# Layer A of a two-layer attention kernel: fillers between the score visits in another order, the output stage two groups later, the next segment's layer norms in the first groups, exp of q read from SBUF

## The chip, the cores and the metric

The kernel runs on one core of a Trainium2 chip. The core has five engines that run side by side, each with its own instruction queue in program order: TensorE (PE in the profile; its weight loads are shown apart as PEld), VectorE (DVE), ScalarE (ACT), GpSimd (POOL) and SyncE (SP, which here only issues DMAs). The metric is the device time of one execution in microseconds (us), lower is better. Verdicts compare medians of several runs.

## The reference

Four layers in a row, A, B, A, B, each with a residual, on x of 2048 tokens by 640 features:

```
x = x + A(layernorm(x));  x = x + B(layernorm(x));  x = x + A(layernorm(x));  x = x + B(layernorm(x))
```

Layer A has 32 heads of 20 features. The tokens are cut into N = 4 segments of 512. Within a segment it is causal softmax attention; across segments there is a memory M, z that is read with phi(q) and updated with phi(k):

```
phi = lambda t: jnp.where(t > 0, t + 1.0, jnp.exp(t))
for s in range(N):
    p = _softmax(qs @ ks^T * scale + mask)
    a_dot = p @ vs
    a_mem = (phi(qs) @ M) / (phi(qs) @ z + 1e-06)
    o = g * a_mem + (1.0 - g) * a_dot
    M = M + phi(ks)^T @ vs ;  z = z + sum(phi(ks))
return o @ wo
```

Layer B is a recurrent-memory attention of 64 small steps. The change does not touch it.

## The kernel before

`layer_A` is called twice. It works through 4 segments (n) of 8 groups of four heads (G); the group counter is g = 8 n + G, from 0 to 31, with two more rounds to drain. Only the instructions of TensorE are held in the order in which the program writes them (`_OrdNC` with the engine "tensor"); the order on ACT, DVE and POOL is the tile scheduler's, which goes by the program's order where several instructions are ready. Tiles of a pool are given out as they come free.

**Score visits.** The heads of a group are done in two pairs p (`half`), and each pair in two visits (`ph`), so a group has four quarters (slots 0 to 3): a visit and then a few fillers. A visit works on up to three PSUM tiles of pool `psx` (three tiles of two banks, tag x):

- S tiles: the causal scores q k^T of the pair, for the row maximum alone. `s_mask` writes the mask with a product of the identity matrix, `s_mm` adds q k^T, `s_max` (line 400, DVE) reduces to the negated maximum `a_nm`. S0 has 1024 elements a partition, S2 512, and S1 768 and 256 in two reduces.
- T tiles: the scores once more, transposed and with the maximum subtracted (`a_q` holds q with the maximum in two extra rows), for the pair three places earlier (tp = p - 3). `t_round` does the products, `t_exp` (line 442, ACT) the exp into `a_PT`, and line 444 (POOL) clears what lies above the diagonal. T0 and T1 have 1024 elements, T2 512.

The products of a pair have 32 rows of contraction, at rows 32 j; the S pair and the T pair of a visit lie on different rows. Visits before: S0, T0, S2 and then T1, S1, T2.

**Fillers.** They do the rest of the layer for neighbouring groups. All their PSUM tiles come from pool `pg`, tag pg, which has two tiles, so a third product in a quarter needs the first to have been copied out.

- `proj_q` (QP): q of the next group; ACT copies it to `a_qT` (line 294); from segment 1 on also exp of q (`a_EQ`, line 298), and DVE makes phi(q) (lines 300, 302).
- `proj_kv` (KV0, KV1): k and v of the next group in two halves; ACT casts them to `a_Kn` and `a_vaug` (line 315). `k_turn` (KT): transpose of k; ACT copies it to `a_kT` (line 323). The S products of the next group need `a_kT`.
- `q_with_max` (Q2): q with the maxima; ACT copies it to `a_q` (line 416).
- `phi_k`: exp of k on ACT (line 332), POOL and DVE make `a_phik`. `state_up` (UP, segments 0 to 2): phi(k)^T v, evacuated on DVE (line 366, `a_upm`), added on POOL. `state_num` (NUM, segments 1 to 3): phi(q) M, copied by ACT to `a_nsb` (line 347).
- `pv` (PV): probabilities times v; ACT copies it to `a_osb` (line 459); `norm` puts the group's output into `a_Onat`.
- The output stage of the segment before, one block of 128 tokens a group in groups 2 to 5: `out_stage_a` (load of x, transpose `a_otps`, copy by ACT to `a_oT`, line 261) and `out_stage_b` in two halves (product with wo, `a_YP`, five matmuls of 320 columns; DVE adds x, line 275; after the second half two stores, line 278 and 281).
- For the next segment, for each of its four blocks: `seg_load` (DMA of x, line 231), `seg_norm` (layer norm: `layernorm_tile`, lines 76 to 83, on DVE with one power on POOL), `seg_tr` (transpose `a_tps`, copied by ACT, line 249). `seg_step` says in which (group, slot) each of the three is done.

Loads of x and stores of the result all go through SP's queue, in order. The output stage of the last segment runs after the loop.

Of the kernel before, what the change touches and what calls it, by code (L numbers as in the profile page):

```python
# [160 lines left out]
def layer_A(nc, tc, C, W, x_src, x_dst, src_is_bf16, nseg=4, out_bf16=False, xb_dst=None, load_w=None, side_loads=None):  # L161
# [6 lines left out]
    with ExitStack() as ctx:  # L168
# [116 lines left out]
        def proj_q(g):  # L285
            n, G = divmod(g, 8)
            s_ = GS[g] = {}
            xnT = SEG[n]["xnT"]
            wqG = W.wq[:, :, 4 * G:4 * G + 4, :].rearrange("p c h s -> p c (h s)")
            QP = pg.tile([128, 512], F32, name="a_QP", tag="pg")  # L290
            for c in range(NCH):
                nc.tensor.matmul(QP[:], lhsT=wqG[:, c, :], rhs=xnT[:, c, :], start=(c == 0), stop=(c == NCH - 1))
            qT = qp3.tile([128, 512], BF16, name="a_qT")
            nc.scalar.copy(qT[:], QP[:])
            s_["qT"] = qT
            if n >= 1:
                EQ = w1.tile([128, 512], BF16, name="a_EQ")
                nc.scalar.activation(out=EQ[:], in_=QP[:], func=ACT.Exp)
                rq = w1.tile([128, 512], BF16, name="a_rq")
                nc.vector.tensor_scalar(out=rq[:], in0=qT[:], scalar1=0.0, scalar2=None, op0=ALU.max)  # L300
                phiq = wk.tile([128, 512], BF16, name="a_phiq")
                nc.vector.scalar_tensor_tensor(out=phiq[:], in0=EQ[:], scalar=1.0, in1=rq[:], op0=ALU.min, op1=ALU.add)
                s_["phiq"] = phiq
# [14 lines left out]
        def k_turn(g):  # L318
            KT_ = pg.tile([128, 4, 128], BF16, name="a_KT", tag="pg")
            for tt in range(4):  # L320
                nc.tensor.transpose(KT_[:, tt, :], Kn[g % 2][:, tt, :, :].rearrange("p j s -> p (j s)"), C.identb[:])
            kT = qp4.tile([128, 512], BF16, name="a_kT")
            nc.scalar.copy(kT[:], KT_[:].rearrange("p t k -> p (t k)"))
            GS[g]["kT"] = kT
# [31 lines left out]
        def state_up(g):  # L356
            n, G = divmod(g, 8)
            s_ = GS[g]
            if n <= nseg - 2:
                UP = pg.tile([128, 128], F32, name="a_UP", tag="pg")  # L360
                pk, va = s_["pk"], s_["va"]
                for tt in range(4):
                    nc.tensor.matmul(UP[:], lhsT=pk[:, tt, :, :].rearrange("p j s -> p (j s)"),
                                     rhs=va[:, tt, :, :].rearrange("p j s -> p (j s)"), start=(tt == 0), stop=(tt == 3))
                upm = w1e.tile([128, 128], F32, name="a_upm")
                nc.vector.tensor_tensor(out=upm[:], in0=UP[:], in1=C.bdmask[:], op=ALU.mult)
                nc.gpsimd.tensor_tensor(out=MZ32[:, G, :], in0=MZ32[:, G, :], in1=upm[:], op=ALU.add)
                nc.gpsimd.tensor_copy(MZb[:, G, :], MZ32[:, G, :])
# [38 lines left out]
        def q_with_max(g):  # L407
            s_ = GS[g]
            N_ = NM[g % 2]
            Q2 = pg.tile([128, 512], F32, name="a_Q2", tag="pg")  # L410
            nc.tensor.matmul(Q2[:], lhsT=C.identb[:], rhs=s_["qT"][:], start=True, stop=False, skip_group_check=True)
            for qc in range(4):
                nc.tensor.matmul(Q2[:, 128 * qc:128 * qc + 128], lhsT=N_[:, qc, :, :].rearrange("p j s -> p (j s)"), rhs=C.identb[:],
                                 start=False, stop=(qc == 3), skip_group_check=True)
            q2 = wk.tile([128, 512], BF16, name="a_q2")
            nc.scalar.copy(q2[:], Q2[:])
            s_["q2"] = q2
# [73 lines left out]
        proj_kv(0, 1)  # L491
        k_turn(0)

        def seg_step(n, G, slot):
            if n + 1 >= nseg:
                return
            for tt, at in enumerate((((0, 0), (0, 2), (0, 3)), ((0, 3), (1, 1), (1, 3)), ((5, 2), (6, 0), (6, 1)), ((6, 0), (6, 2), (6, 3)))):
                for f, w_ in zip((seg_load, seg_norm, seg_tr), at):
                    if w_ == (G, slot):
                        f(n + 1, tt)  # L500

        def filler(g, slot):
            n, G = divmod(g, 8)
            out = n >= 1 and 2 <= G <= 5 and n <= nseg
            if slot == 0:
                if 0 <= g - 1 < NGR:
                    state_up(g - 1)
                if g + 1 < NGR:
                    proj_q(g + 1)
            elif slot == 1:  # L510
                if 0 <= g - 1 < NGR:
                    q_with_max(g - 1)
                if g + 1 < NGR:
                    proj_kv(g + 1, 0)
                if out:
                    out_stage_a(n - 1, G - 2)
            elif slot == 2:
                if g < NGR:
                    phi_k(g)
                    state_num(g)  # L520
                if g + 1 < NGR:
                    proj_kv(g + 1, 1)
                if out:
                    out_stage_b(n - 1, G - 2, (0,))
            else:
                if g + 1 < NGR:
                    k_turn(g + 1)
                if 0 <= g - 2 < NGR:
                    pv(g - 2)
                    norm(g - 2)  # L530
                if out:
                    out_stage_b(n - 1, G - 2, (1,))
            seg_step(n, G, slot)

        for g in range(NGR + 2):
            n, G = divmod(g, 8)
            for half in range(2):
                p, tp = 2 * g + half, 2 * g + half - 3
                for ph in range(2):
                    items = ((("S", 0), ("T", 0), ("S", 2)), (("T", 1), ("S", 1), ("T", 2)))[ph]  # L540
                    todo = []
                    for kind, r in items:
                        if kind == "S" and g < NGR:
                            todo.append((kind, p, r, s_mask(p, r)))
                        elif kind == "T" and 0 <= tp < 2 * NGR:
                            todo.append((kind, tp, r, t_tile()))
                    for kind, p_, r, X in todo:
                        (s_mm if kind == "S" else t_round)(p_, r, X)
                        (s_max if kind == "S" else t_exp)(p_, r, X)
                    if g < NGR and half == 1 and ph == 1:  # L550
                        negmax_rows(g)
                    filler(g, 2 * half + ph)
            if side_loads is not None and n == 0:
                if G == 0:
                    build_gates(nc, st, W, side_loads[1])
                side_loads[0](G, GS[g]["kT"])
# [671 lines left out]
```

## Time and profile before

| | |
|---|---|
| median of 3 runs | 2793.08 us (2786.16 to 2794.82) |
| the profiled execution | 2787.25 us, span 2785.5 us |
| mean granted TensorE clock | 0.981 |
| first A layer | about 0 to 405 us of the span |
| second A layer | about 1390 to 1790 us |

A group of layer A takes 8.4 to 14 us in segment 0, 9.7 to 12 us in segments 1 and 2, and 9.2 to 11.7 us in segment 3. The profile has a page (shares of each engine, the span in 40 slices, the chain that ended last, groups of instructions by line) and answers on parts of the trace: the busy time of each engine in a window, who waited for whom, and the instructions in order of time. Busy time of PE is modelled, since matmuls are pipelined; the start times are measured. A line "PE a_otps <- ACT a_q" in the list of waits says that the instruction of PE which writes a_otps was held until the instruction of ACT which writes a_q was done.

### The profile page before, as it was taken

The numbers are of one execution on the slowest core, as the hardware profiler recorded it, in microseconds if no ns is written. First come the engines' busy times: TensorE is split into PE (matmuls) and PEld (weight loads), VectorE is DVE, ScalarE is ACT, GpSimd is POOL, SyncE is SP. The second block draws the span as 40 slices with busy tenths as digits, with TensorE's granted clock in tenths as the row PEclk, the third lists the DMA queues.
The fourth block names the chain that finished last, engine by engine and source line by source line (L and its number), as shares of the span: only waits on it lengthen the run. The fifth ranks groups of instructions, "written<-read, shape, count | busy, mean of one in ns | idle before, by whom it ended". The sixth has DMA issues, their size and how long they took to land. (4 is left out here: it accounts for less than half of the span.)

```text
span 2785.5 us, 146956 instructions
## 1 busy us (share of the span) xinstructions
PE 2574.7 (92%) x65414; PEld 1700.1 (61%) x65480; DVE 1686.6 (61%) x4553; ACT 1584.9 (57%) x3708; POOL 715.2 (26%) x1645
## 2 busy tenths in 40 slices
PE   5888879999999999999978888799999999999998
PEld 3555556666666666666645555556666666666665
DVE  6888854555555555555578888445555555555554
ACT  4888854555555555544458888445555455555443
POOL 4666541111111111111146665411111111111110
PEclk9999979999999999999989999899999999999999
DMA  6111162221212212111120111721211121211110
GB/s 239 41 44 40 30 195 69 45 46 41 45 43 45 43 43 45 43 39 30 41 99 28 51 49 37 231 47 39 42 42 40 40 44 40 43 41 38 39 26 20
DMA packets 322300, 156.36 MB, mean 56 GB/s; under 512 B 245760, under 2 KB 310400, under 8 KB 318592
## 3 DMA queue, kind: packets, MB, share of 16 engines
q1 hardware_dynamic: 320224, 136.47, 19.2%
q8 instruction: 512, 8.39, 1.3%
q10 hardware_dynamic: 1440, 10.49, 1.0%
q14 instruction: 124, 1.02, 0.1%
HBM read 95.15 MB, written 51.71 MB: 53 GB/s over the span
## 5 line engine op out<-in xcount | busy, mean ns | idle before, releaser
L101 PEld LDWEIGHTS <-b_HX 128*32 128x32 bf16 x15360 | 430.2, 97 | 341.0 <-issue 14.1
L101 POOL TENSOR_TENSOR b_Pm<-b_E,b_rs 128x96 bf16<-128x96 bf16 x128 | 63.3, 495 | 1443.2 <-ACT b_Vth L101 1094.2
L400 DVE TENSOR_REDUCE a_nm<-a_S 128x2 f32<-128x1024 f32 (+3 forms) x512 | 396.5, 815 | 51.4 <-PE a_T L101 26.6
L442 ACT ACTIVATE a_PT<-a_T 128x1024 bf16<-128x1024 f32 (+1 forms) x384 | 325.4, 889 | 84.9 <-PE a_T L101 50.6
L101 PE MATMUL b_OPS<-b_wo,b_OTsb 128*32 128x320 bf16 x8192 | 308.0, 301 | 10.3 <-issue 8.5
L101 PEld LDWEIGHTS <-b_OTsb 128*32 128x32 bf16 x8192 | 200.5, 97 | 97.0 <-DVE b_OTsb L101 24.1
L101 DVE CAST b_HX<-b_MT 128x8 bf16<-128x8 f32 x372 | 63.7, 172 | 277.5 <-PE b_MT L101 272.2
L444 POOL TENSOR_SCALAR_AFFINE_SELECT a_PT<-a_PT 128x256 bf16<-128x256 bf16 (+1 forms) x384 | 193.5, 520 | 143.2 <-ACT a_PT L442 141.0
L101 ACT CAST b_msb<-b_OPS 128x64 bf16<-128x64 f32 x378 | 69.3, 256 | 237.7 <-PE b_OPS L101 237.7
L101 ACT CAST b_kq<-b_Kb 128x512 bf16<-128x512 f32 x128 | 74.9, 585 | 201.6 <-PE b_Kb L101 201.6
L101 DVE COPY b_KT<-b_TPak 128x128 bf16<-128x128 bf16 x128 | 28.8, 225 | 227.0 <-PE b_TPak L101 227.0
L101 PE MATMUL b_Va<-b_wv,b_HX 128*32 128x512 bf16 x2520 | 160.8, 380 | 0.0
L101 PE MATMUL b_Vb<-b_wv,b_HX 128*32 128x512 bf16 x2520 | 160.1, 379 | 0.0
L101 PEld LDWEIGHTS <-b_kq 128*128 128x128 bf16 x2080 | 116.8, 98 | 68.8 <-ACT b_kq L101 55.6
L101 PE MATMUL b_Ka<-b_wk,b_HX 128*32 128x512 bf16 x2520 | 158.8, 379 | 0.0
L101 DVE TENSOR_SCALAR b_kq<-b_Qa 128x512 bf16<-128x512 f32 x128 | 88.5, 691 | 115.9 <-PE b_Qa L101 112.9
L101 PE MATMUL b_Kb<-b_wk,b_HX 128*32 128x512 bf16 x2520 | 158.6, 379 | 0.0
L101 PE MATMUL b_Qb<-b_wq,b_HX 128*32 128x512 bf16 x2520 | 158.6, 379 | 0.0
L101 PE MATMUL b_Qa<-b_wq,b_HX 128*32 128x512 bf16 x2520 | 158.6, 379 | 0.0
L101 DVE CAST b_OTsb<-b_OTP 128x160 bf16<-128x160 f32 (+1 forms) x384 | 122.3, 374 | 39.6 <-PE b_OTP L101 39.6
L101 PE MATMUL b_vtail<-b_wv,b_TX 128*32 128x256 bf16 x2880 | 137.7, 271 | 6.6 <-issue 3.5
L101 ACT ACTIVATE b_E<-b_SP 128x320 bf16<-128x320 f32 (+1 forms) x256 | 81.1, 368 | 109.0 <-PE b_Va L101 95.3
(195 smaller groups left out, 5764.8 us busy)
## 6 DMA issues: line engine op xcount, KB each, us to landing
b_QKd<-b_tu SPq DMA_DIRECT2D x128, 128.0 KB
b_tl<-b_QKd SPq DMA_DIRECT2D x128, 128.0 KB
b_wv<-in_B_Wv_dram SPq DMA_DIRECT2D x10, 1024.0 KB
b_wo<-in_B_Wo_dram SPq DMA_DIRECT2D x16, 640.0 KB
b_VTd<-b_vt SPq DMA_DIRECT2D x256, 32.0 KB
b_Vth<-b_VTd SPq DMA_DIRECT2D x512, 16.0 KB
b_XO<-xres SPq DMA_DIRECT2D x256, 30.0 KB
b_wk<-in_B_Wk_dram ACTq DMA_DIRECT2D x5, 1024.0 KB
```

The costliest lines, as they stand in the source:

```text
L101: r = f(*a, **k)
L400: nc.vector.tensor_reduce(out=nm[:, qc, 2 * pr:2 * pr + 2], in_=X[:, :, o:o + w_], axis=AX.X, op=ALU.max, negate=True)
L442: nc.scalar.activation(out=PT[:, :, b:b + width], in_=Y[:, :, 0:width], func=ACT.Exp, scale=SC)
L444: nc.gpsimd.affine_select(out=dv, in_=dv, pattern=[[0, 2], [0, diag], [1, 128]], compare_op=ALU.is_ge, fill=0.0, base=0, channel_multiplie ...
```

## The change

Four things, all in layer A:

1. The fillers are named items in a table. UP moves from slot 0 to slot 2, in front of KV1; NUM moves behind KV1. The output stage moves from slots 1, 2, 3 (transpose, first half, second half) to slots 0, 1, 3; the transpose stands ahead of QP.
2. The output stage runs in groups 4 to 7 (`OUT_LAG = 4`), not 2 to 5.
3. Loads, norms and transposes of the next segment's four blocks have other places (`TPS`): three blocks are finished in groups 0 to 2, the fourth in group 5; before, two in groups 0 and 1 and two in groups 5 and 6.
4. The visits take their tiles in another order, S0, S2, T0 and S1, T2, T1 (`VISITS`), and all products of a visit are written ahead of its reduces and exps. The branch for kind "X" is not used by this table.

Apart from that, exp of q reads the bf16 copy in SBUF in place of the fp32 product in PSUM.

```diff
@@ -295,7 +295,7 @@
             s_["qT"] = qT
             if n >= 1:
                 EQ = w1.tile([128, 512], BF16, name="a_EQ")
-                nc.scalar.activation(out=EQ[:], in_=QP[:], func=ACT.Exp)
+                nc.scalar.activation(out=EQ[:], in_=qT[:], func=ACT.Exp)
                 rq = w1.tile([128, 512], BF16, name="a_rq")
                 nc.vector.tensor_scalar(out=rq[:], in0=qT[:], scalar1=0.0, scalar2=None, op0=ALU.max)
                 phiq = wk.tile([128, 512], BF16, name="a_phiq")
@@ -491,62 +491,70 @@
         proj_kv(0, 1)
         k_turn(0)
 
+        TPS = (((0, 0), (0, 1), (0, 2)), ((0, 0), (0, 3), (1, 1)), ((0, 2), (1, 2), (2, 0)), ((1, 0), (5, 1), (5, 3)))
+        SLOTS = (('otps', 'QP'), ('Q2', 'KV0', 'YP0'), ('UP', 'KV1', 'NUM'), ('KT', 'PV', 'YP1'))
+        VISITS = (('S0', 'S2', 'T0'), ('S1', 'T2', 'T1'))
+        OUT_LAG = 4
+
         def seg_step(n, G, slot):
             if n + 1 >= nseg:
                 return
-            for tt, at in enumerate((((0, 0), (0, 2), (0, 3)), ((0, 3), (1, 1), (1, 3)), ((5, 2), (6, 0), (6, 1)), ((6, 0), (6, 2), (6, 3)))):
+            for tt, at in enumerate(TPS):
                 for f, w_ in zip((seg_load, seg_norm, seg_tr), at):
                     if w_ == (G, slot):
                         f(n + 1, tt)
 
+        def item(what, g):
+            no, Go = divmod(g - OUT_LAG, 8)
+            out = no >= 1 and Go < 4
+            if what == "UP" and 0 <= g - 1 < NGR:
+                state_up(g - 1)
+            elif what == "QP" and g + 1 < NGR:
+                proj_q(g + 1)
+            elif what == "Q2" and 0 <= g - 1 < NGR:
+                q_with_max(g - 1)
+            elif what in ("KV0", "KV1") and g + 1 < NGR:
+                proj_kv(g + 1, int(what[2]))
+            elif what == "NUM" and g < NGR:
+                phi_k(g)
+                state_num(g)
+            elif what == "KT" and g + 1 < NGR:
+                k_turn(g + 1)
+            elif what == "PV" and 0 <= g - 2 < NGR:
+                pv(g - 2)
+                norm(g - 2)
+            elif what == "otps" and out:
+                out_stage_a(no - 1, Go)
+            elif what in ("YP0", "YP1") and out:
+                out_stage_b(no - 1, Go, (int(what[2]),))
+
         def filler(g, slot):
-            n, G = divmod(g, 8)
-            out = n >= 1 and 2 <= G <= 5 and n <= nseg
-            if slot == 0:
-                if 0 <= g - 1 < NGR:
-                    state_up(g - 1)
-                if g + 1 < NGR:
-                    proj_q(g + 1)
-            elif slot == 1:
-                if 0 <= g - 1 < NGR:
-                    q_with_max(g - 1)
-                if g + 1 < NGR:
-                    proj_kv(g + 1, 0)
-                if out:
-                    out_stage_a(n - 1, G - 2)
-            elif slot == 2:
-                if g < NGR:
-                    phi_k(g)
-                    state_num(g)
-                if g + 1 < NGR:
-                    proj_kv(g + 1, 1)
-                if out:
-                    out_stage_b(n - 1, G - 2, (0,))
-            else:
-                if g + 1 < NGR:
-                    k_turn(g + 1)
-                if 0 <= g - 2 < NGR:
-                    pv(g - 2)
-                    norm(g - 2)
-                if out:
-                    out_stage_b(n - 1, G - 2, (1,))
-            seg_step(n, G, slot)
+            for what in SLOTS[slot]:
+                item(what, g)
+            seg_step(g // 8, g % 8, slot)
 
         for g in range(NGR + 2):
             n, G = divmod(g, 8)
             for half in range(2):
                 p, tp = 2 * g + half, 2 * g + half - 3
                 for ph in range(2):
-                    items = ((("S", 0), ("T", 0), ("S", 2)), (("T", 1), ("S", 1), ("T", 2)))[ph]
                     todo = []
-                    for kind, r in items:
-                        if kind == "S" and g < NGR:
-                            todo.append((kind, p, r, s_mask(p, r)))
+                    for what in VISITS[ph]:
+                        kind, r = what[0], int(what[1])
+                        if kind == "X":
+                            X = s_mask(p, r) if g < NGR else t_tile()
+                            if g < NGR:
+                                todo.append(("S", p, r, X, 0))
+                            if 0 <= tp - 1 < 2 * NGR:
+                                todo.append(("T", tp - 1, r, X, 256))
+                        elif kind == "S" and g < NGR:
+                            todo.append((kind, p, r, s_mask(p, r), 0))
                         elif kind == "T" and 0 <= tp < 2 * NGR:
-                            todo.append((kind, tp, r, t_tile()))
-                    for kind, p_, r, X in todo:
-                        (s_mm if kind == "S" else t_round)(p_, r, X)
-                        (s_max if kind == "S" else t_exp)(p_, r, X)
+                            todo.append((kind, tp, r, t_tile(), 0))
+                    for step in range(2):
+                        for kind, p_, r, X, o0 in todo:
+                            f = (s_mm, s_max)[step] if kind == "S" else (t_round, t_exp)[step]
+                            f(p_, r, X, *((o0,) if o0 else ()))
                     if g < NGR and half == 1 and ph == 1:
                         negmax_rows(g)
                     filler(g, 2 * half + ph)
```

## What is predicted, and how it is worked out

> **What bounds the kernel.** I read the page first: shares of the engines, then the 40 slices.
>
> ```profile
> PE 2574.7 (92%) x65414; PEld 1700.1 (61%) x65480; DVE 1686.6 (61%) x4553; ACT 1584.9 (57%) x3708; POOL 715.2 (26%) x1645
> ...
> PE   5888879999999999999978888799999999999998
> ...
> DVE  6888854555555555555578888445555555555554
> ACT  4888854555555555544458888445555455555443
> ```
>
> Each slice is 69.6 us. Slices 1 to 5 and 21 to 25 are the two A layers (about 400 us each). There PE, DVE and ACT all stand at 8 tenths: no engine is full, so they wait on one another. The rest is layer B, PE at 9 tenths, and the change does not touch it.
>
> Next, the busy time by group. I cut at the first key transpose (a_KT) of each group, found in the timeline. The rows are: a group of segment 0 with no extra work, one of segment 1 with the output stage (out group), one with two layer norms, one of segment 2 with neither (plain), one of the last segment (plain).
>
> ```profile
> 77.56:85.93 8.37, 8.07 (x124) 5.20 (x123) 5.64 (x11) 7.53 (x16) 5.48 (x13) 1.00 0.01 2
> 139.14:151.09 11.95, 9.79 (x142) 6.60 (x141) 9.62 (x19) 9.48 (x18) 7.73 (x16) 1.00 0.17 57
> 186.12:196.96 10.84, 8.67 (x132) 5.75 (x132) 10.67 (x26) 8.84 (x18) 8.53 (x16) 1.00 0.06 17
> 196.96:206.70 9.74, 8.85 (x127) 5.68 (x126) 9.10 (x19) 8.92 (x20) 7.41 (x15) 1.00 0.01 2
> 294.86:304.06 9.20, 8.43 (x123) 5.37 (x123) 8.05 (x17) 8.58 (x19) 5.61 (x12) 1.00 0.18 2
> ```
>
> Columns: length, then PE, PEld, DVE, ACT, POOL. A plain group has 0.6 to 0.8 us of idle ACT: ACT nearly bounds it. A group with two norms has DVE at 10.67 of 10.84. An out group has over 2.3 us idle on every engine, and there are 12 a layer. That is what the waits of PE in the first A layer name (total, times, longest):
>
> ```profile
> PE a_otps L101 <- ACT a_q L416: 11.4, 12, 1.0
> ...
> PE a_YP L101 <- ACT a_kT L323: 7.8, 12, 0.7
> PE a_tps L101 <- ACT a_kT L323: 6.0, 7, 1.1
> ...
> PE a_YP L101 <- ACT a_nsb L347: 5.1, 12, 0.5
> ```
>
> The reason is in the timeline of an out group. All filler products share two PSUM tiles (pool pg). A quarter (a visit and its fillers) with three of them stops PE until the first has been copied out, and ACT does that copy after the exps of the visit:
>
> ```profile
> 220.51 1.81 DVE L400 TENSOR_REDUCE a_nm<-a_S 128x2 f32<-128x1024 f32 x2
> ...
> 222.24 0.28 DVE L366 TENSOR_TENSOR a_upm<-a_UP,c_bd 128x128 f32<-128x128 f32 x1
> ...
> 222.80 1.52 ACT L442 ACTIVATE a_PT<-a_T 128x1024 bf16<-128x1024 f32 x2
> ...
> 224.18 0.62 ACT L416 CAST a_q<-a_Q 128x512 bf16<-128x512 f32 x1
> ...
> 224.85 0.44 PE L101 MATMUL a_otps<-c_identb,a_Onat 128*128 128x128 bf16 x5 [0.95 <-ACT a_q L416]
> ...
> 227.38 0.84 PE L101 MATMUL a_YP<-a_wo,a_oT 128*128 128x320 bf16 x5 [0.42 <-ACT a_nsb L347]
> ```
>
> The score products of the four quarters start at 219.89, 222.09, 225.45, 228.38 and 231.84: 2.20 + 3.36 + 2.93 + 3.46 = 11.95 us.
>
> **The change, by parts** (differences per group; t counts from a quarter's first score product).
>
> *Output transpose to quarter 0, first half of the output product to quarter 1.* In quarter 0 the transposes (0.28 us from start to next start) replace UP (0.23), and both tiles are free there: its 0.95 us stall goes. ACT then runs exp 0.5 to 1.5, the output copy (0.69 a row, 0.65 after overlap) to 2.15, the copy of q to 2.7, exp of q to 3.2. Before, ACT stood idle until QP ended and reached this point at about 3.0, so 0.2 of the copy is new. In quarter 1 YP0 is now the third product: exps to 4.65, copy of q2 to 5.2, YP0 at 5.25. The stall comes back whole, on a product of 0.69 instead of 0.28 us. Masks 0.32: next scores at 6.2 against 2.20 + 3.36 = 5.56, **+0.6**.
>
> *UP to quarter 2, NUM after KV1.* YP0 and its 0.42 stall leave; UP (0.23 to 0.66) comes; KV1 ends at 1.4; NUM is a third product. Its tile comes free by the copies of KV1 (exp to 1.55, two casts to 2.1) or by upm, which DVE does behind the two reduces (1.82 + 0.28: 2.5). The tile pool decides which; I take the earlier. NUM 2.15 to 2.4, masks, second visit at 2.7 (before 2.93). Quarter 3 keeps YP1 and its wait for kT, 3.45. **-0.2**, or +0.25 by upm. So an out group of segments 1 and 2 gets +0.4 (bounds -0.3, if ACT takes nsb without a gap, to +1.0, both slow ends). 16 of them: **+6.4**. In the last segment there is no UP: quarter 2 is bound by the reduce of S0 (about 2.0), which cancels the +0.6: 8 groups at 0 (-0.4 to +0.3).
>
> *The same in plain groups.* QP ends 0.23 earlier without UP, and the ACT gap of 0.45 in front of the copy of q shrinks by that; in quarter 2 NUM waits for the casts and ACT loses about 0.3 in front of nsb and the exps. +0.1 each (-0.25 to +0.5), 16 groups of segments 1 and 2: **+1.6**. The later UP itself delays nothing: its sum is read a segment later.
>
> *Score visits.* Per visit the same products, reduces and exps. S0, T0 and S2 take tiles as they come free; T0 now stands behind S2 in program order, and S2 uses the array rows of S0. Cost 0, because row groups run side by side: here the S products start before the T products ahead of them in the program (T 128, T 384, S 384 was the order):
>
> ```profile
> 201.79 0.34 PE L101 MATMUL a_S<-a_kT,a_qT 32*128 32x384 bf16 x2
> 201.84 0.32 PE L101 MATMUL a_T<-a_q,a_kT 32*128 32x384 bf16 x2
> ```
>
> In the second visit S1 comes ahead of T1 and the short exp (T2, 0.55) ahead of the long one: the first tile is free 0.5 us earlier, but S0's product follows S2's masks and waits for the second tile (1.3 to 1.5 either way). Bound from the good side 0.1 a visit; I take 0.
>
> [...]
>
> *Exp of q from SBUF.* Rows: 603 ns from PSUM (512 elements). From SBUF only a_EK: 0.50 us for 320; the PSUM copies of 336 and 512 (0.43, 0.58) give 0.85 ns an element, so 0.66. +0.06 x 48 exps = 2.9 if all lie on ACT's path, 0 if none; QP's tile comes free one exp earlier, which nothing waits for in these rows. I take **+1.5**.
>
> *Layer norms and their transposes.* A norm costs DVE 1.75 to 1.9 us (2 x 0.48, 0.20, 0.14, 0.45 or 0.61). Before: two in groups 0 and 1, two in group 6. After: three in groups 0 to 1.5, one in group 5, an out group, where DVE has 2.3 us to spare. Before, a segment pays 0.96 (group 0: 10.70 in place of 9.74), about 0.2, 1.1 (10.84) and 0.5: 2.8. After: three norms 3.0 (each past 0.64 us of slack a group, scaled to the 1.2 measured for two), and the transpose in quarter 1 of group 1 is a third product like otps (+0.75 over quarter 3, where the next scores wait for kT anyway): 3.9 in all. +1.1 x 4 segments = **+4.5** (-5 to +12). In segment 0 the early extra norm (1.8) and the two gone from group 6 (1.5 net) cancel. In the first layer DVE waits 1.53 us at 30.49 for the load of the next segment's x; asked a quarter earlier it waits longer, and the reduces queue behind it: **+1.5** (0 to 4).
>
> *Queues.* The same DMAs (three of the output stage, four loads) leave by SP, 0.33 to 0.42 us each; the later loads now go ahead of the output stores and not behind them. DMA share 0.17 in out groups: 0.
>
> **Sum:** 6.4 + 0 + 1.6 + 1.5 + 4.5 + 1.5 = **+15.5 us**. The profiled execution took 2787.25 (span 2785.5), the median is 2793.08 (2786.16 to 2794.82). That gives 2803 on the one and 2809 on the other; I say **2806**.
>
> **Rivals.**
> 1. *Faster: the output stage is hidden.* ACT's order in layer A is the scheduler's, not the program's. If the q2 copy stands ahead of an exp, or the exps of the second visit start as soon as S1 goes first, YP0 finds its tile, and the waits 11.4 + 5.1 of a layer go: 2 x 16.5 = 33, **2760**. For it: 2.3 us idle on all engines there, and the norms leaving group 6. Against: in every quarter of these rows exps go before copies. It decides once the copy of q2 ends 1 us earlier.
> 2. *Much slower: NUM waits for upm.* 32 groups x 0.45 = 14 on top, and three norms make groups 0 and 1 DVE-bound without hoisting (+8): +38, **2830**. For it: an early row has Q2 waiting 2.25 us for upm while QP's tile was free. Against: there DVE was late by a norm.
> 3. *No change:* stalls only change places: **2793**.
> 4. *PE starts in order:* T0 behind S2, 0.11 us in 128 visits: +14 on the sum, **2820**.
>
> **Chances:** forecast 0.39, rivals 0.35, 0.11, 0.10, 0.05. About 0.3% (8.4 us) is what a measurement of this kernel can tell from no change. Faster by more: 0.35 (rival 1); same: 0.10; slower: 0.39 + 0.11 + 0.05 = 0.55. The range takes in rival 1 and rival 2 with some spread: 2756 to 2842; for the likeliest alone 2795 to 2825 (unknown costs on one side or the other).
>
> **What would show it.** Waits of PE: a_otps for a_q gone, a_YP for a_q about 12 x 1.1 a layer, a_YP for a_nsb gone, a new wait of a_NUM (for a_vaug: forecast; for a_upm: rival 2). Out groups at 12.3 us in segments 1 and 2 and 11.7 in the last; a group 6 without norms near 9.8; group 0 at 12 or more. a_EQ at 0.66. T0 products starting with S0's (if 0.2 later: rival 4). The prediction is wrong if out groups fall under 11.5, or if layer A's groups without output move by more than 0.5.

## The result and the profile after

| | before | after |
|---|---|---|
| median of 4 runs each | 2789.62 us (2785.36 to 2794.82) | 2829.99 us (2826.39 to 2836.65) |
| ratio, 95% interval | | 1.0147 [1.0118, 1.0175] |
| span of the profiled execution | 2785.5 us | 2824.7 us |
| mean granted TensorE clock | 0.981 | 0.977 |

The kernel is slower by 40.4 us, and the spans of the two profiled executions differ by 39.2. The page of the changed kernel: busy time of the engines, then the 40 slices (70.6 us each).

```profile
PE 2601.4 (92%) x65480; PEld 1707.7 (60%) x65480; DVE 1683.1 (60%) x4553; ACT 1595.9 (56%) x3708; POOL 711.5 (25%) x1645
...
PE   5878878999999999999978778799999999999998
...
DVE  6777864555555555555578778545555555555554
ACT  3878863555555455554448788545545555555543
```

DVE and ACT are as busy as before to within 4 and 11 us. PE is busy 26.7 us longer, although the change adds no product: that is a first hint that its products run more slowly somewhere (66 records of products are missing in the page of before, too few to make the difference). Layer A fell from 8 tenths to 7 in places; layer B is as it was.

Cut at the first key transpose of each group, as in the prediction, the loss is found in few places (us, from the first cut of a segment to the first cut of the next; segment 0 begins at its second cut, and the last segment ends at its eighth group):

| | segment 0 | 1 | 2 | 3 |
|---|---|---|---|---|
| first A layer, before | 77.2 | 90.1 | 88.7 | 74.4 |
| first A layer, after | 86.0 | 100.7 | 96.2 | 72.9 |
| second A layer, before | 73.2 | 92.3 | 88.8 | 74.5 |
| second A layer, after | 68.2 | 98.4 | 96.3 | 72.9 |

Segments 1 and 2 of both layers give 31.7 of the 39.2 us, segment 0 of the first layer 8.8. What is left cancels: group 0 of the layers, which lies ahead of the first cut of the table, the rest of segment 0 of the second layer, and the last segments with their drain.

Groups of the changed kernel (length, then PE, PEld, DVE, ACT, POOL with their counts, then the granted clock, the DMA share and GB/s): one of segment 0 while layer B's weights are loaded, one of segment 1 with no extra work, an out group with a norm and transposes, a plain group, an out group, and a plain one of the last segment.

```profile
75.28:88.64 13.36, 10.53 (x125) 6.32 (x123) 7.08 (x12) 8.48 (x15) 5.85 (x15) 0.86 0.44 158
151.13:163.55 12.42, 9.51 (x129) 6.11 (x127) 8.60 (x18) 9.01 (x17) 8.02 (x17) 0.86 0.01 2
190.18:205.63 15.45, 11.12 (x148) 7.12 (x147) 11.76 (x24) 10.50 (x20) 8.41 (x18) 0.96 0.17 55
251.66:262.36 10.70, 8.69 (x129) 5.53 (x127) 8.67 (x17) 9.09 (x17) 7.18 (x15) 1.00 0.01 2
275.82:288.52 12.70, 10.16 (x143) 6.70 (x141) 9.73 (x19) 9.63 (x18) 7.79 (x16) 1.00 0.15 53
343.61:352.77 9.16, 8.64 (x125) 5.31 (x123) 7.89 (x16) 8.57 (x17) 5.98 (x11) 1.00 0.01 3
```

The plain group took 9.74 before and takes 10.70, with no engine busier by more than 0.17 us (ACT, 8.92 to 9.09): DVE had 0.64 us idle there and has 2.03. The out group went from 11.95 to 12.70. The plain group of the last segment, where phi(k) and UP are not done, stayed (9.20, 9.16). And some groups now run at a granted clock of 0.86 to 0.96, where every group of segments 1 to 3 had 1.00 before.

The waits of PE in the first A layer of the changed kernel (total, times, longest):

```profile
PE a_S L101 <- DVE a_nm L400: 24.0, 25, 3.2
...
PE a_YP L101 <- ACT a_q L416: 12.8, 11, 1.3
PE a_NUM L101 <- ACT a_vaug L315: 9.8, 17, 0.6
PE a_T L101 <- DVE a_nm L400: 6.7, 5, 1.5
```

The waits of a_otps for a_q and of a_YP for a_nsb are gone; those on the second and third lines are the ones that were forecast for them. The first line is the news: before, the score masks waited 8.3 us in all (17 times, longest 1.8) for the reduces of DVE. They now wait 24.0. The last line, T products that wait for a reduce, is hardly larger than before (5.6 us in 9 waits), but it lies elsewhere: all five waits are in segment 0, where the kernel before had three.

**Where the reduces become late.** The timeline of the changed kernel around the cut at 251.66 (start, length, engine, line, operation; the bracket is the idle time of that engine before it, and who ended it; lines in between are left out at the dots):

```profile
250.88 0.45 POOL L367 TENSOR_TENSOR a_MZ<-a_MZ,a_upm 128x128 f32<-128x128 f32 x1 [0.19 <-DVE a_upm L366]
...
251.21 0.34 PE L101 MATMUL a_S<-a_kT,a_qT 32*128 32x384 bf16 x2
...
251.40 0.29 POOL L368 CAST a_MZb<-a_MZ 128x128 bf16<-128x128 f32 x1
...
251.66 0.45 POOL L333 TENSOR_SCALAR a_EK<-a_EK 128x320 f32<-128x320 f32 x1
...
252.15 0.49 DVE L335 SCALAR_TENSOR_TENSOR a_phik<-a_Kn,a_EK 128x320 bf16<-128x320 bf16 x1 [1.35 <-POOL a_EK L333]
...
252.86 0.94 DVE L400 TENSOR_REDUCE a_nm<-a_S 128x2 f32<-128x768 f32 x1
...
254.29 0.27 PE L101 MATMUL a_S<-c_negu,c_identb 128*128 128x128 bf16 x2 [1.13 <-DVE a_nm L400]
...
255.08 1.02 ACT L442 ACTIVATE a_PT<-a_T 128x1024 bf16<-128x1024 f32 x1 [1.06 <-PE a_S L101]
```

phi(k) of a group, which its UP needs a group later, is a chain ACT (exp, a_EK), POOL (clamp, line 333), DVE (a_phik, line 335). UP of the group before, now in quarter 2, brings an add and a cast to POOL (lines 367 and 368; "the two adds" below), and the clamp stands behind them. On DVE a_phik stands ahead of the reduces of S1. So DVE waits 1.35 us for POOL. S1's first scores are there from about 251.55 (251.21 + 0.34); the last 0.6 us of that wait, a_phik itself (0.49) and a small step of NUM (line 349) stand between them and their reduce, which starts 1.31 us after they end. S1's reduces end late, the next score tile is not free (PE 1.13 us), and ACT has no T product to work on (1.06 us). Before, the same stretch of a plain group has the reduces first and a_phik after them, with no wait; the scores are there at 196.87 (196.54 + 0.33), and the reduce starts 0.57 us later:

```profile
197.44 1.28 DVE L400 TENSOR_REDUCE a_nm<-a_S 128x2 f32<-128x768 f32 x2
...
198.85 0.91 DVE L335 SCALAR_TENSOR_TENSOR a_phik<-a_Kn,a_EK 128x320 bf16<-128x320 bf16 x1
```

**Segment 0 of the first layer.** The timeline of the changed kernel there:

```profile
79.76 1.28 DVE L400 TENSOR_REDUCE a_nm<-a_S 128x2 f32<-128x768 f32 x2
...
81.09 0.39 PE L101 MATMUL a_T<-a_q,a_kT 32*128 32x128 bf16 x4 [1.48 <-DVE a_nm L400]
```

T1 is now the last of its visit. By this wait, the tile that it is given is the one that S1 of the same visit used: it starts when S1's reduce ends (79.76 + 1.28 = 81.04). PE has nothing to do for 1.48 us. The kernel before has a wait of this kind too, for T2, which was last there:

```profile
77.34 0.28 PE L101 MATMUL a_T<-a_q,a_kT 32*128 32x256 bf16 x2 [1.43 <-DVE a_nm L400]
```

It came three times in this segment before (at 55.61, 66.81 and 77.34, 1.43 us each). Now T1 waits five times (1.21 to 1.48 us), in some groups twice. Group 2 (16.01 us in place of 12.12) has another cause beside it: DVE waits 3.39 us for a load of x, and the masks 3.21 us for the reduces behind it. PE's clock after the pauses is in the last section.

### The profile page after: what moved, and what is told of

The parts are those of the page before. It is cut to its first block, busy times and chain, and to the rows that moved or that the text cites. A ratio compares the mean times of both kernels' runs of the same rounds, so it can differ in the third digit from the quotient of the medians.

```text
span 2824.7 us, 147039 instructions
## 1 busy us (share of the span) xinstructions
PE 2601.4 (92%) x65480; PEld 1707.7 (60%) x65480; DVE 1683.1 (60%) x4553; ACT 1595.9 (56%) x3708; POOL 711.5 (25%) x1645
## 4 chain that ended last, share of the span: by engine, by line
PE 53%; DVE 5%; ACT 4%; POOL 1%; DMA 1%; issue 1%; SPq 0%; ACTq 0%; DVEq 0%; POOLq 0%
PE b_OPS L101 8%; PE b_tail L101 4%; PE b_Ka L101 4%; PE b_Kb L101 4%; PE b_Qb L101 4%; PE b_Qa L101 4%; PE b_Va L101 4%; PE b_Vb L101 3%; PE b_SP L101 3%; DVE a_nm L400 3%; PE b_OTP L101 3%; ACT a_PT L442 2%; PE b_PTP L101 2%; PE b_OPSd L101 2%; PE b_vtail L101 2%
## 5 line engine op out<-in xcount | busy, mean ns | idle before, releaser
L400 DVE TENSOR_REDUCE a_nm<-a_S 128x2 f32<-128x1024 f32 (+3 forms) x512 | 403.4, 808 | 35.9 <-PE a_S L101 23.5
L444 POOL TENSOR_SCALAR_AFFINE_SELECT a_PT<-a_PT 128x256 bf16<-128x256 bf16 (+1 forms) x384 | 205.9, 540 | 164.2 <-ACT a_PT L442 162.8
L101 PE MATMUL a_S<-c_negu,c_identb 128*128 128x128 bf16 (+1 forms) x768 | 110.1, 242 | 43.1 <-DVE a_nm L400 36.1
L101 PEld LDWEIGHTS <-c_identb 128*128 128x128 bf16 x1088 | 93.7, 99 | 91.7 <-issue 78.4
```

Source lines behind the costliest of these rows:

```text
L101: r = f(*a, **k)
L400: nc.vector.tensor_reduce(out=nm[:, qc, 2 * pr:2 * pr + 2], in_=X[:, :, o:o + w_], axis=AX.X, op=ALU.max, negate=True)
L444: nc.gpsimd.affine_select(out=dv, in_=dv, pattern=[[0, 2], [0, diag], [1, 128]], compare_op=ALU.is_ge, fill=0.0, base=0, channel_multiplie ...
```

## The experiments

The times of all runs are beside the kernel before on the same chip: its median was 2791.24 us for the first four, 2790.78 for the next four, 2791.62 for the next four and 2791.17 for the last two. Segment sums are those of the profiled execution.

### Undoing parts of the change

**e1: phi(k) behind S1's reduces on DVE.** The DVE part of phi(k) is written in quarter 3 and ordered behind the last reduce (an order, not a wait).

```diff
+        def phi_k2(g):   # DVE part of phi_k alone
+            r = nc.vector.scalar_tensor_tensor(out=pk[...], in0=KNv, ..., in1=EK[:], ...)
+            tc.add_manual_dep(r.ins, LASTMAX["i"].name, ..., reason="order")
-        SLOTS = (..., ('KT', 'PV', 'YP1'))
+        SLOTS = (..., ('PHK', 'KT', 'PV', 'YP1'))
```

> The changed kernel with one order fixed: on DVE the instruction that writes a_phik is held behind the two reduces of S1 (in the trace of the changed kernel it stands ahead of them and waits 1.35 us for the clamp of a_EK on POOL). Theory A (DVE stands still behind POOL in quarter 3, the reduce of S1 and the next scores behind it, about 0.8 us in each of the 32 groups of segments 1 and 2): 2803 to 2812 us, plain groups of segment 2 back from 10.70 to about 9.8 us. Theory B (the third product of quarter 2, NUM waiting 0.57 us for a_vaug, is what costs): no change, 2822 to 2836, plain groups at 10.6 or more. Theory C (the new order of the visits costs): no change either.

2811.94 us, ratio 1.0079 [1.0052, 1.0105]: about 18 of the 40 us come back. Segments 1 and 2 of the first layer went from 100.7 and 96.2 to 93.4 and 91.6. The waits of the score masks fell from 24.0 to 18.1 us, and DVE no longer waits for POOL in front of a_phik (34.6 us over both layers in the changed kernel, 15.6 before). Windows of this run, the group that had 12.42 us at a clock of 0.86, a plain group and an out group:

```profile
148.81:158.97 10.16, 8.65 (x127) 5.48 (x126) 9.11 (x18) 8.97 (x17) 8.33 (x17) 1.00 0.01 2
242.06:252.05 9.99, 8.72 (x127) 5.57 (x127) 8.95 (x18) 8.97 (x17) 7.44 (x15) 1.00 0.01 3
263.75:276.15 12.40, 9.76 (x143) 6.62 (x142) 10.13 (x20) 9.63 (x18) 7.82 (x16) 1.00 0.16 55
```

So the order on DVE is worth 0.7 us in a plain group (10.70 to 9.99) and 0.3 in an out group (12.70 to 12.40), and up to 2.3 where the clock fell as well. Over segments 1 and 2 of both layers it returns 17.9 of the 31.7 us. Segment 0 of the first layer stayed at 85.7: the theory explains only one of the two places.

**e2: UP back in quarter 0, NUM ahead of KV1.**

```diff
-        SLOTS = (('otps', 'QP'), ('Q2', 'KV0', 'YP0'), ('UP', 'KV1', 'NUM'), ...)
+        SLOTS = (('UP', 'otps', 'QP'), ('Q2', 'KV0', 'YP0'), ('NUM', 'KV1'), ...)
```

> The changed kernel with UP back in quarter 0 and NUM back in front of KV1; the rest of the change stays. Theory A: the adds of UP on POOL leave the stretch in which the clamp of a_EK has to run, so a_phik is not late: 2800 to 2812, plain groups of segment 2 at 9.7 to 9.9. Theory B: the same 2800 to 2812, since NUM has its tile at once. Theory C: 2822 to 2836.

2824.66 us, 1.0116 [1.0091, 1.0142], which misses the expectation. Plain groups are at 9.7 again, but out groups are at 13.6: quarter 0 now has three products for two tiles. This run can't tell the theories apart, since it takes one wait away and brings another.

**e3: the old order of visits.**

```diff
-        VISITS = (('S0', 'S2', 'T0'), ('S1', 'T2', 'T1'))
+        VISITS = (('S0', 'T0', 'S2'), ('T1', 'S1', 'T2'))
```

(and products and reduces or exps of a visit written one after the other, as before)

> The changed kernel with the old order within the visits (S0, T0, S2 and T1, S1, T2, each reduce or exp written behind its product); the rest stays. Theories A and B: 2820 to 2836, plain groups of segment 2 still over 10.4. Theory C: 2795 to 2810, plain groups at 9.8. Apart from these: groups 2 and 3 of segment 0 in the first layer, 13.3 us each with T1 waiting 1.2 to 1.5 us for the reduce of S1, should come back to 10.5 to 11.2 if the order of the visits is their cause (5 us of the total).

2811.29 us, 1.0074 [1.0052, 1.0097]: another 19 us. Segment 0 of the first layer falls from 86.0 to 74.5, its groups 3 and 4 (counted from 0) from 13.3 and 13.4 to 9.33 each; segments 1 and 2 only by 4.1 and 1.5. The time lies between the two expectations; the plain group (10.46) is as theories A and B had it, and groups 3 and 4 fell further than expected. The edit restores two things, the order of the tiles and the writing of each reduce or exp behind its products; which of them matters was not tried.

**e4: the old places of norms, transposes and output stage.** `TPS` as before, `OUT_LAG = 2`.

> The changed kernel with the old places of the next segment's loads, norms and transposes and with the output stage in groups 2 to 5; fillers, visits and exp of q stay as changed. Theories A, B, C: 2815 to 2824 (the two groups of over 15 us in segment 1 go, and DVE's wait of 3.4 us for a load of x in the first layer). If the moved norms and output stage are the main cause: 2790 to 2805.

2845.28 us, 1.0190 [1.0167, 1.0213]: slower than the change itself, where 2815 to 2824 was expected. With the new fillers the first out group of a segment takes 13.9 to 15.6 us, in the last segment too (14.15 and 15.04), which has no norms and transposes. The wait in it is this one:

```profile
247.62 0.23 PE L101 MATMUL a_otps<-c_identb,a_Onat 128*128 128x128 bf16 x1 [2.20 <-POOL a_Onat L478]
```

The output transpose, now in quarter 0, needs the output of the last group of the segment before, and with the output stage in group 2 that output is only just being written by POOL. PE waits 17.6 us in 8 times for it in e4 and 3.5 in 2 in the changed kernel; the difference, 14.1, is of the size of the 15 us, though other places gain and lose too (segment 0 of the first layer went from 86.0 to 90.5). So the later output stage (`OUT_LAG = 4`) spares the new fillers this wait: in company with them, this part of the change is a gain, not a cost.

**e5: e1 and e3 together.**

> Both edits that each gained some 18 us on the changed kernel, together: a_phik held behind the reduces of S1 on DVE, and the old order within the visits. If they take away two separate losses (one in segments 1 and 2, one in segment 0 of the first layer): 2790 to 2800 us, segment 0 of the first layer at 74 to 77 us and segments 1 and 2 at some 185 us in each layer. If both only loosen one and the same place: 2806 to 2814.

2794.54 us, 1.0003 [0.9989, 1.0018]: equal to before. The two gains nearly add up (18 and 19 us alone, 35 together); the losses are two, in two places.

**e6: the old table of fillers, all else as changed.**

```diff
-        SLOTS = (('otps', 'QP'), ('Q2', 'KV0', 'YP0'), ('UP', 'KV1', 'NUM'), ('KT', 'PV', 'YP1'))
+        SLOTS = (('UP', 'QP'), ('Q2', 'KV0', 'otps'), ('NUM', 'KV1', 'YP0'), ('KT', 'PV', 'YP1'))
```

> The changed kernel with the old table of fillers (UP and QP; Q2, KV0 and the output transpose; NUM, KV1 and the first half; KT, PV and the second half); the output stage stays in groups 4 to 7, and norms, visits and exp of q as changed. If the table of fillers carries the loss of segments 1 and 2: groups with output at 11.9 to 12.2, plain groups at 9.7 to 10, total 2798 to 2808 with segment 0 of the first layer still at 83 or more. If the visits carry it: 2818 or more.

2799.26 us, 1.0029 [1.0013, 1.0044]. Segments 1 and 2 stand at 92.1 and 89.9, near before; segment 0 of the first layer keeps 84.4. The fillers make the loss of segments 1 and 2, and most of that of segment 0 is not theirs.

### Parts of the change alone, in the kernel before

**e7: the new visits alone.**

> The kernel before with the new order within the visits alone. If that order by itself costs what its undoing gained: 2800 to 2812 us, most of it in segment 0 of the first layer, where T1 waits for the reduce of S1. If the order is harmless without the other parts: 2786 to 2795.

2796.74 us, 1.0018 [1.0007, 1.0029]; segment 0 of the first layer 77.2 to 83.5, segments 1 and 2 of that layer +2.1 and +0.6; in the second layer segments 0 and 1 fell by 3.1 and 2.2. The time is between the two expectations.

**e8: norms, transposes and output stage in their new places, alone** (`TPS` and `OUT_LAG = 4`).

> The kernel before with the new places of loads, norms and transposes and the output stage in groups 4 to 7, nothing else. My sum had +6 us for it (2796 to 2800). Undoing it in the changed kernel cost 15 us, so a gain by itself is the rival: 2772 to 2784.

2785.03 us, 0.9981 [0.9969, 0.9993]: faster than before by 2 to 9 us, just short of the rival's range, and the fastest of all kernels here, by less than single runs of the kernel before differ. Segments 1 and 2, where +1.1 us each was forecast, moved by +0.6 and -0.3 in the first layer and -0.4 and -0.4 in the second.

**e9: the new table of fillers alone** (the inverse of e6's edit).

> The kernel before with the new table of fillers alone (UP in quarter 2, NUM behind KV1, output stage in quarters 0, 1, 3, still in groups 2 to 5). Theory A (the fillers bring a_phik ahead of the reduces of S1 on DVE, whatever the visits): plain groups of segments 1 and 2 at 10.4 or more, groups with output at 12.5, total 2808 to 2822. If the loss needs the new visits as well: 2790 to 2800.

2827.85 us, 1.0126 [1.0111, 1.0142]: +35 us, more than expected and nearly the size of the whole loss. A plain group takes 10.03, out groups 12.6, and the first out group of a segment 12.7 to 16.6: the output stage is in groups 2 to 5 here, so the wait of e4 is in it (PE waits 14.9 us in 8 times for a_Onat, 2.4 in 2 before). That part of the 35 us is not in the changed kernel. DVE waits 40.3 us for POOL in front of a_phik.

**e10: exp of q from SBUF alone.**

> The kernel before with exp of q read from SBUF alone. My term was +1.5 us (0 to 2.9): 2790 to 2795. The row of a_EQ at 0.63 us against 0.60. If the scheduler's order on DVE and ACT shifts with it: 2797 or more.

2796.23 us, 1.0016 [1.0006, 1.0025]: +4.5 us (1.7 to 7). A row of it takes 630 ns in place of 603, which over 48 exps is 1.3 us. Out groups went from 11.95 to 12.1.

**e12: UP to quarter 2 and NUM behind KV1 alone,** the output stage in its old slots.

```diff
-        SLOTS = (('UP', 'QP'), ('Q2', 'KV0', 'otps'), ('NUM', 'KV1', 'YP0'), ...)
+        SLOTS = (('QP',), ('Q2', 'KV0', 'otps'), ('UP', 'KV1', 'NUM', 'YP0'), ...)
```

> The kernel before with UP moved to quarter 2 in front of KV1 and NUM behind KV1, nothing else (the output stage stays in quarters 1, 2, 3, so quarter 2 of an out group has four products). Plain groups of segments 1 and 2 alone matter here: theory A 10.2 to 10.7 us with a wait of DVE in front of a_phik, theory B (the wait of NUM alone, hidden by ACT) 9.8 to 10.0. Total 2805 to 2825.

2806.16 us, 1.0057 [1.0040, 1.0074]: +16. A plain group goes from 9.74 to 10.28, as theory A has it. DVE waits 40.3 us in front of a_phik here too, out groups are at 12.3.

Alone, the parts cost 35 (fillers), 5 (visits), 4.5 (exp of q) and -5 (norms and output stage): 39.5 together, against 41 measured for the whole (0.0147 x 2790). The agreement is chance: the 35 hold the wait for a_Onat that the change does not have, and inside the change the visits cost 19.

### The chain of phi(k), and the clock

**e11: POOL's clamp ahead of UP's adds.** All of the next group's phi(k) (exp, clamp and a_phik) is written in quarter 2, behind NUM and so a group earlier than in the change, and the two adds of UP are ordered behind its clamp.

```diff
+            elif what == "PHN" and g + 1 < NGR:
+                phi_k(g + 1)
+            elif what == "MZ" and 0 <= g - 1 < NGR:
+                state_mz(g - 1)      # the two adds on POOL, behind the clamp
-        SLOTS = (..., ('UP', 'KV1', 'NUM'), ...)
+        SLOTS = (..., ('UP', 'KV1', 'NUM', 'PHN', 'MZ'), ...)
```

> The changed kernel with one order on POOL turned round: the clamp of a_EK for the next group ahead of the two instructions that add UP into the state (a_MZ, a_MZb). If DVE's wait of 1.35 us in front of a_phik is POOL working off those two first, the wait falls to about 0.7 and the total to 2814 to 2824; plain groups of segment 2 from 10.7 to some 10.1 to 10.4. If POOL is not the reason: 2826 to 2836.

2808.95 us, 1.0062 [1.0045, 1.0079]: 21 us less than the change, more than expected. On DVE a_phik still stands ahead of S1's reduces; its wait for POOL fell from 34.6 to 21.2 us, in the plain group from 1.35 to 0.76, and that group from 10.70 to 10.24. The wait can be loosened at either of its ends, POOL's queue or DVE's, with about the same gain (21 and 18 us).

**e13 and e14: does the clock add to the waits?** In segment 0 of the first layer the two products of T2 are written nine times, into the same tile with the same values, so that PE works where it would wait for S1's reduce. e13 is that in the changed kernel, e14 in the kernel of e3, where PE has no such wait.

```diff
+            again = 9 if r == 2 and g < 8 and src_is_bf16 else 1
-            for n_, (kc, o, w_) in enumerate(parts):
+            for n_, (kc, o, w_) in enumerate(parts * again):
```

> The changed kernel; in segment 0 of the first layer the two products of T2 are written nine times in place of once (the same values into the same tile), so that PE works while it would wait for the reduce of S1. No wait is taken away: T1 still comes after that reduce, and T2's exp comes up to 0.9 us later. Theory (the clock answers to PE's idle time): the half-clock stretches in groups 2 to 5 of that segment go; those four groups hold 10.2 us of length times (1 - clock) in the changed kernel (16.01 at 0.75, 13.29 at 0.78, 13.36 at 0.86, 9.23 at 0.84), and the segment falls from 86.0 by 3 to 7 us although work was added. Rival (the waits themselves are the loss, the clock follows the loads of layer B's weights or is harmless): the segment stays at 86 or grows by up to 16 visits x 0.9 = 14 us, clock as before.

> The same added products in the changed kernel with the old order of visits (2811.3 us, segment 0 of the first layer 74.5 us, groups 3 and 4 at 9.33 with a clock of 1.00): there PE has no such wait and no lost clock to win back in these groups. Both theories: the segment grows by the price of the products, 16 visits x 0.3 to 0.9 us = 5 to 14 us. If it stays at 74.5 the products are free there too, and a gain in the other run is the clock's alone; if it falls, the added products act in some other way than by the clock.

e13: 2829.13 us, 1.0145 [1.0122, 1.0169]; e14: 2816.63 us, 1.0090 [1.0068, 1.0113]. The segment as a whole answers to neither theory of e13: 86.7 us, where 79 to 83 was expected by the one. That of e14 grew from 74.5 to 84.4, as both theories had it. Groups 3 and 4 of e13:

```profile
65.32:76.18 10.86, 10.78 (x155) 7.44 (x155) 6.61 (x11) 8.09 (x16) 4.80 (x13) 0.90 0.52 195
76.18:86.88 10.70, 10.31 (x155) 7.12 (x155) 7.10 (x13) 8.18 (x16) 5.44 (x15) 1.00 0.54 199
```

Group 4 of e3 and of e14, the one without and the other with the added products:

```profile
68.52:77.85 9.33, 8.39 (x124) 5.36 (x123) 7.15 (x12) 8.00 (x16) 5.61 (x15) 1.00 0.64 224
```

```profile
72.97:83.21 10.24, 9.53 (x155) 6.86 (x155) 7.40 (x13) 8.21 (x16) 5.66 (x15) 1.00 0.56 206
```

Where PE does not wait, the products cost 0.9 us a group (9.33 to 10.24, both at full clock). In the changed kernel the same products make group 4 2.66 us shorter (13.36 at a clock of 0.86 to 10.70 at 1.00) and group 3 2.43 (13.29 at 0.78 to 10.86 at 0.90). But e13 does not part the clock from the waits. Its expectation said that no wait is taken away, and the trace shows the opposite. In group 4 the products of T2 and T1 (22 records) run without a pause from 80.50 to 81.88, while the reduces of S1 end at 81.85: T1 does not wait for them any more, so it must have got another tile. From 62 us on no T product waits for a reduce in this segment, where the changed kernel has four such waits (5.3 us). Group 4 gained 2.66 us and paid about 0.9 for the added products, 3.6 in all; its two waits (1.48 and 1.21 us) are 2.7 of that, which leaves 0.9 for the clock.

A pair of groups of e7 says a little more. Both have two waits of this kind: group 3 (1.52 and 1.21 us) took 11.75 us at full clock, group 4 (1.39 and 1.21) took 12.55 at a clock of 0.86. By this one pair, which is not an experiment, a half-clock stretch costs some 0.8 us there. So the clock does add to the loss, by an estimate of 0.8 to 0.9 us a stretch, and the waits themselves are the larger part.

In groups whose clock was full already the added products only cost (groups 6 and 7: 10.24 to 10.76, 9.16 to 10.21), and group 2, which holds the load of layer B's weights and a wait for x, went from 16.01 to 18.80; its wait for x grew from 3.39 to 5.41 us. The control lost in that group as well (13.3 to 16.75), for a reason that these runs do not show.

## Why the prediction was half right

The direction, the waits that would go and those that would come were right; the size was not: +15.5 us forecast, about +40 measured. By its own steps:

- **Output stage to quarters 0, 1, 3: right within 0.1 us.** Forecast: otps's stall goes, YP0 waits about 12 x 1.1 us a layer for the copy of q2. Measured: gone, and 12.8 us in 11 waits. Out groups were to be 12.3 us; the changed kernel has 12.70, but with a_phik back in its place (e1) 12.40, so the other 0.3 is the next point's. In the last segment 11.7 was forecast and 11.79 measured.
- **UP to quarter 2, NUM after KV1: the failing step.** The prediction costed PE and the two PSUM tiles, took the shorter branch for NUM (behind KV1's casts), and that branch is what came: 9.8 us in 17 waits for a_vaug, none for upm. But it ended with "The later UP itself delays nothing: its sum is read a segment later", +0.1 for a plain group. That holds for the sum and not for the queue it passes: UP's two adds are on POOL ahead of the clamp, the clamp is what a_phik waits for, and a_phik is ahead of S1's reduce. The plain group cost +0.96 (10.70 against 9.74), of which e1 returns 0.7, and the out group +0.75, of which it returns 0.3. The term for plain groups of segments 1 and 2 should have been about 13 us in place of 1.6 (the 16 groups without output there went from 167.4 to 180.4 us in all, norms included), that for out groups 19 in place of 6.4 (192.5 to 211.3). By the prediction's own sign (groups without output that move by more than 0.5) it was wrong here. The view that could have told it, DVE's 15.6 us of waiting for POOL in front of a_phik, was in the trace of before: the chain had already no slack in 19 groups.
- **Order of visits: 0 was wrong in one place.** T0 starts with S0 as forecast: in the changed kernel the rows of S0, T0 and S2 start at 254.50, 254.51 and 254.72, so the fourth rival (a wait of T0 behind S2) did not happen. T0, which stands behind S2 in the program, starts 0.21 us ahead of it there; those two products are on different rows of the array. What was missed is the second visit in segment 0 of the first layer: the bound of "1.3 to 1.5 either way" for a tile was given for S0, not for T1, which is now last and can get S1's own tile (five waits of 1.21 to 1.48 us, where T2 had three of 1.43). Alone this costs 5 us (e7); inside the change, with its other waits, e3 gets 19 back.
- **Norms, transposes: wrong in sign.** +4.5, and +1.5 for the load of x in the first layer, were forecast; alone the step, with the later output stage that had no term, gives -2 to -9 us (e8). The waits of the norms for x did grow, as forecast, from 5.8 us in 6 waits to 12.3 in 9 in the first layer. The charge of 3.9 us a segment was too dear (its two terms, 3.0 and 0.75, give 3.75), since segments 1 and 2 of e8 hardly moved. What was left out is that with the old output stage the output transpose in quarter 0 would wait for a_Onat: e4 shows 13.9 to 15.6 us for that group.
- **Exp of q: the row right, the sum too small.** 0.63 us measured, 0.66 estimated, against 0.603: 1.3 us over 48 exps. Alone the edit costs 4.5 (1.7 to 7). The later end of the exp moves something else by a little; which was not tried.
- **The clock had no term.** The prediction took the granted clock of before for every group. After, twelve more stretches of half clock lie in the two layers (last section). In the first layer e1 takes those of segments 1 and 2 away, and e3 those of groups 3 to 5 of segment 0, together with the waits; what all of them cost in time is not known, one in segment 0 some 0.8 to 0.9 us by the estimate above.
- **The rivals.** The second named 2830 us, which is the time, by a mechanism that did not happen: NUM does not wait for upm. That number is a coincidence, and so is that the time lies inside the wide range, which rival 2 had stretched. Its other half, "three norms make groups 0 and 1 DVE-bound", does not hold either (e8). The first rival, faster by hidden copies, fails at the row that was to decide it: YP0 still waits for the copy of q2, 1.09 us in the out group at 275.82. Its premise of over 2.3 us idle on every engine of an out group was 2.16 for PE (11.95 less 9.79).

What stays open: why the new visits cost four times as much inside the change (19 us) as alone (5 us). Half-clock stretches may be a part of it. Open too is how the 8.8 us of segment 0 divide into waits of T1, the wait for x and the clock.

## What to carry to other kernels

When a step moves to another place in the program, follow its results on every engine that it touches, and ask on each queue what it now stands in front of: the product that was moved cost PE nothing, and its two small adds on POOL held up a clamp, which held up DVE, which held up PE. Where the order of an engine is the scheduler's, a moved step also changes which of two ready instructions goes first; an order that matters (the reduces that free PSUM tiles ahead of work that is not due) is better written down. Parts that need each other should be priced together: the output transpose in quarter 0 costs a wait for the last group's output unless the output stage also runs later. And a wait of PE may be followed by a lower clock: of the eight waits of 1.21 to 1.48 us of T1 or T2 for a reduce in segment 0 of the first layer (three before, five after the change), three were followed by a clock of 0.50 that had been 1.00.

## What the runs showed of the hardware

**A clock of 0.50 after some of PE's pauses.** The windows around the pause of 1.48 us in segment 0 in the changed kernel (columns as above, the clock is the third number from the end):

```profile
80.50:81.00 0.50, 0.00 (x0) 0.00 (x0) 0.50 (x2) 0.00 (x0) 0.24 (x1) 1.00 1.09 459
...
81.80:82.40 0.60, 0.60 (x7) 0.58 (x6) 0.00 (x0) 0.60 (x1) 0.00 (x0) 0.50 0.10 27
...
84.80:85.20 0.40, 0.40 (x8) 0.31 (x7) 0.40 (x1) 0.16 (x1) 0.00 (x0) 0.94 0.87 164
```

PE is idle from 79.61 to 81.09, 1.48 us; from about 81.4 to 84.85 the granted clock is 0.50, and products that took 0.39 us take 0.61 (a_Q at 69.70 and at 81.42). The pause of 1.21 us that ends at 88.16 is followed by a clock of 0.50 too, from 88.27 to 91.68. A pause alone does not decide it: after those of 1.39 and 1.21 us that end at 69.38 and 74.96 the clock stays at 1.00, and of the three pauses of 1.43 us in the kernel before, which end at 55.61, 66.81 and 77.34, only the first is followed by half clock (55.75 to 59.16). The earliest of the five waits of T1 in the changed kernel, which ends at 61.45 (1.39 us), lies inside a stretch of half clock that had begun at 57.55. What decides it was not shown: no run changed the pauses alone.

Length times (1 - clock), summed over the 31 groups between the cuts of each layer, is 10.2 us before, all of it in segment 0, and 30.7 after. The stretch above, from 81.44 to 84.85 at 0.50, makes 1.7 of it; counted in stretches like that one, it is six before and 18 after. How much of the difference of 20.5 us lies on the path is not known, since PE does not bound every quarter; e1, which takes only a wait of DVE away, brings segments 1 and 2 of the first layer from 6.9 to 0.0 (those of the second only from 5.0 to 3.5).
